# Loading v one chunk of four batches at a time from the GpSimd queue, in a fused linear-attention and SoLU kernel

## The chip, the cores and the metric

The kernel runs on one core of one Trainium2 chip. The core has five engines that run their own instruction lists and wait for each other by semaphores: TensorE (PE, matmuls; its weight loads are shown as PEld), VectorE (DVE), ScalarE (ACT), GpSimd (POOL) and SyncE (SP, which here only issues transfers). Sixteen DMA engines move data between the memory of the chip (HBM) and the on-chip memory (SBUF). The metric is the device time of one execution in microseconds (us).

## The reference

Two parts, one after the other. The first is a linear attention with decay, for 4 batches, 8 heads, 768 positions and a head size of 48; the second is a feed-forward layer with a softmax-gated unit and a layer norm, on the 3072 rows of 384 values that the first gives.

```python
for t in range(S):
    kt, vt, rt, wt = (k[:, :, t], v[:, :, t], r[:, :, t], w[:, :, t])
    cur = np.einsum('bhd,bhe->bhde', u[None] * kt, vt)
    y[:, :, t] = np.einsum('bhd,bhde->bhe', rt, state + cur)
    state = wt[:, :, :, None] * state + np.einsum('bhd,bhe->bhde', kt, vt)
...
h = x @ w_in
sm = e / (np.sum(e, axis=-1, keepdims=True) + 1e-09)     # e = exp(h - max)
solu = h * sm
ln = (solu - mu) / np.sqrt(var + 1e-06) * g_ln
return (ln @ w_out).astype(np.float32)
```

The arrays r, k, v and w are fp32 of shape (4, 8, 768, 48). For one batch and one chunk of 128 positions, v is 128 x 8 x 48 values, or 196,608 bytes, and lies in HBM in runs of 48 values (192 bytes), one for each position and head.

## The kernel before

The 768 positions are cut into 6 chunks of 128, and one chunk of one batch is a *unit*: unit i is batch i mod 4 of chunk i div 4, 24 units in all. A unit goes through some forty steps, and the whole program is one list, ORDER, in which each word is a step with its unit: `vb9.a` is the step `vb` of unit 9, on ACT (`.p` is POOL, `.d` is DVE; a digit is the PSUM bank). Each engine issues its own steps in the order of that list (the class `InOrder`), so an engine that waits for one step holds up all its later ones, whatever they need.

The steps that matter here, by their words:

- `LW`, `LK`, `LR`, `LV`: SP loads w, k, r and v of one unit, four transfers of 1024 runs of 192 bytes. Each goes into one of seven tiles (`NIO`), whose rows hold a head's 48 values in 64 places. `LI`, `LO` load the two weight matrices, `out` stores a finished unit; SP issues these too, 127 transfers in all.
- `vb` (function `v_cast`): casts a unit's v to bf16, on POOL for 12 units, on ACT for 6 and on DVE for 6. The bf16 tiles `vb` are a ring of ten.
- `p`, `q`, `qh` (POOL) and `dg` (DVE): the products of r, k and u, summed over a head. `dv` (POOL) is that sum times v.
- `lw` (ACT), `cum` (PE), `ex` (ACT), `kp` (DVE), `krk`, `krr` (PE), `kr`: k and r with their decays, turned for the matmuls.
- `M` (PE), `m` (ACT or DVE), `sel` (POOL, for the m that ACT copied): the scores of a unit and their mask. `Y` (PE) multiplies them with v; `y` copies the result, on DVE with dv added.
- `S` (PE) and `st` (DVE): the state that a batch's next chunk needs; S reads the cast v.
- `X`, `H` (PE), `e` (ACT), `he` (DVE), `ea` (POOL), `hq`, `Oa`, `Ob` (PE), `sq` (ACT), `qm` (DVE), `lv` (ACT, two instructions: the logarithm and the exponential that make 1/sqrt), `o`: the second part.
- `gw`, `mn`, `mc`, `ce`: the scaling and centring of the second weight matrix, once, at some 27 to 43 us.

The words are laid out so that several units are under way on every engine at once. Units are not taken strictly in sequence: at the start unit 2 goes first, then 1, 0, 3, 4.

Of the kernel before, what the change touches and what calls it, by code (L numbers as in the profile page):

```python
# [8 lines left out]
F32 = mybir.dt.float32  # L9
BF16 = mybir.dt.bfloat16  # L10
# [11 lines left out]
LW2 LU0 ik0 lw2 hot5.4 cum2.0 LW1 lw1 us0.7 ih0 LW3 lw3 cum3.2 LR2 uc0 ex2 LK2 p2 LV2 vb2.p kp2 hot4.4 krk2.6 krr2  # L22
LR1 LK1 cum1.4 LW0 ex1 kp1 kr2.d hot1.0 S2.7 lw0 et2 LV1 vb1.d LW4 st2 p1 q1 hot2.0 krk1.1 krr1 q2 qh2 dg2 LG0
kr1.a M2.4 ex3 hot1.0 M1.6 m1.d dv2 LR0 LK0 p0 q0 cum0.0 ex0 lw4 cum4.6 ex4 kp0 krk0.1 krr0 LR3 gs0.0 gc0 dg1
m2.d Y2.i0 kr0.d LK3 p3 LR4 LV0 vb0.a dg0 dv1 kp3 Y1.i5 hot3.1 krk3.4 krr3 LK4 kp4 M0.2 m0.d krk4.1 y1.a X1.5
krr4 y2.a X2.0 dv0 xT2.d hot1.6 Y0.n7 y0.d kr3.a M3.2 hot1.0 X0.6 S1.4 p4 q3 kr4.a xT1.a xT0.a LI2 LI1 wi1.a
M4.0 m4.a et1 LI0 S0.5 et0 wi0.d m3.d LO1 wi2.p H1.6 e1 gw5.a H2.0 e2 H0.2 LO0 gw2.a q4 qh4 dg4 qh3 dg3 gw4.p
gw7.p LV3 vb3.p dv3 sel4 LW6 e0 gw6.d st1 LV4 vb4.p he1 lw6 dv4 gw1.d LW5 gw0.d gw3.d mn0.4 mc0 ce5.p ce6.p
Y3.i7 ce4.p he2 st0 he0 cum6.0 y3.a ce7.p hot1.5 X3.6 lw5 xT3.a ce3.d LK6 LR6 p6 Y4.n5 LR5 LK5 ce2.d hq0.a ex6
LW7 cum5.2 H3.6 p5 y4.d ex5 ce1.d ce0.d Oa0.5 kp6 krk6.1 krr6 S4.0 hq1.d Oa1.4 kp5 krk5.3 krr5 X4.2 Ob1 e3 he3  # L30
LV5 q6 q5 kr5.d hq2.a et4 st4 M5.6 kr6.a M6.0 xT4.d lw7 cum7.2 hq3.a sq1 m6.a m5.d dg5 vb5.d qm1 dv5 Ob0 ex7 sq0
qm0 S3.7 qh6 LR7 LK7 p7 kp7 et3 lv1 st3 lv0 H4.0 Y5.n6 y5.d LR9 LK8 o1.d e4 krk7.3 krr7 Oa2.2 he4 X5.7 q7 kr7.d
LW9 lw9 o0.a LK9 p9 LW8 lw8 S5.6 et5 cum9.4 ex9 Ob2 sq2 LR8 p8 st5 dg6 kp9 qm2 LV6 xT5.a LV9 vb6.p dv6 sel6
cum8.0 ex8 kp8 hq4.a LV7 LV11 out1 LW10 dg7 vb7.p dv7 Oa3.3 vb9.a lv2 H5.6 e5 M7.4 m7.d he5 q8 krk9.1 LK10 krr9
kr9.a S9.0 et9 Ob3 sq3 st9 q9 qm3 o2.a out0 ea5.p Y6.i5 y6.a LV8 LR10 Y7.n4 y7.d LW11 LW12 krk8.1 M9.6 lw10 lv3
X6.2 xT6.a m9.d o3.a krr8 LV10 out3 out2 kr8.d qh9 dg9 dg8 hq5.d cum10.4 ex10 kp10 S6.0 vb11.d et6 X7.2 xT7.a
st6 p10 vb8.d dv8 dv9 H6.6 e6 he6 H7.2 lw11 e7 he7 M8.4 m8.a Oa5.1 Y9.n0 Ob5 sq5 y9.d cum11.6 ex11 krk10.5 krr10
qm5 kr10.d S7.4 et7 st7 Oa4.3 hq6.d lv5 lw12 o5.a X9.2 sel8 Y8.i0 vb10.p y8.a LK11 LR11 kp11 xT9.d q10 dg10 p11
M10.4 m10.a sel10 S10.1 et10 st10 dv10 S8.0 et8 S11.7 et11 X8.6 xT8.a LK12 LW13 cum12.4 q11 ex12 lw13 st11 st8
Ob4 sq4 qm4 LW14 LR12 kp12 p12 lw14 lv4 o4.a out5 LK13 LV12 LR13 Y10.n2 dg11 y10.d H8.6 e8 krk12.1 krk11.0 krr11  # L40
krr12 kr12.d he8 kr11.a q12 qh12 cum13.4 H9.2 vb12.p S12.1 ex13 p13 q13 ea7.p dg12 kp13 dv11 LW16 LR14 LK14 e9
he9 et12 st12 M12.6 m12.a Oa6.0 X10.5 xT10.a krk13.4 krr13 kr13.a M11.6 m11.d ea8.p dv12 sel12 p14 cum14.2 ex14
q14 out4 Ob6 sq6 hq8.d M13.4 m13.d LV13 hq7.a LW15 lw15 lw16 kp14 vb13.d H10.6 dg13 qm6 LW18 lw18 Y11.n1 y11.d
Oa8.5 LK16 LR15 LR16 LK15 e10 he10 hq9.a krk14.4 Y12.i3 krr14 lv6 qh14 kr14.d p15 ea10.p dv13 LR18 LV14 vb14.p
q15 qh15 LK18 p18 Ob8 sq8 qm8 y12.a S13.2 et13 st13 o6.a lv8 X11.1 xT11.d cum16.6 ex16 X12.3 hq10.d LW19 kp16
Oa9.4 cum15.0 xT12.a Ob9 ex15 kp15 sq9 o8.a dg14 dv14 qm9 M14.2 m14.a sel14 krk16.7 Oa7.6 krr16 kr16.d lv9 o9.d
cum18.0 ex18 kp18 Ob7 LV15 S14.5 et14 st14 krk15.3 krr15 kr15.d LK19 Y13.i2 lw19 cum19.0 krk18.7 p16 q16 vb15.a
S15.4 y13.a sq7 qm7 dg15 X13.5 xT13.d ex19 LR19 kp19 lv7 o7.a q18 krr18 kr18.d H11.2 et15 st15 krk19.5 krr19
kr19.d LW17 lw17 cum17.0 e11 he11 ex17 ea11.p out8 LK17 LR17 p17 kp17 H12.6 e12 he12 hq11.a p19 H13.4 e13 Oa10.3
Y14.n2 M16.0 m16.a dg16 q19 dv15 y14.d ea12.p ea13.p M15.6 m15.d he13 Ob10 sq10 X14.2 out9 Oa11.1 LW20 qm10 lw20  # L50
cum20.6 hq12.d krk17.0 krr17 out6 out7 LV16 vb16.a dv16 xT14.a S16.2 LR20 ex20 LK20 dg18 et16 st16 lv10 o10.a
H14.4 e14 kp20 Ob11 sq11 kr17.d LK23 qm11 lv11 o11.a Oa12.2 krk20.3 krr20 kr20.a he14 sel16 Y16.n7 y16.d Y15.n6
y15.d M19.4 m19.a M18.0 m18.d Ob12 X15.7 xT15.a q17 hq13.d LV19 LW21 LV17 X16.3 xT16.a ea14.p vb19.a M17.4 m17.d
sq12 LK22 out10 qm12 dg17 qh19 vb17.p sel19 p20 hq14.a LW22 LV20 q20 qh20 dv17 M20.0 LV21 m20.d out11 LK21 H15.6
e15 he15 lw22 ea15.p H16.4 LV18 vb18.p dv18 LR21 p21 lw21 Oa14.3 Y17.n1 LR22 LV23 q21 dg19 dv19 Ob14 LR23 p23
p22 e16 he16 lv12 Oa13.0 LW23 o12.a out12 sq14 qm14 hq15.d vb20.a lv14 dg20 dv20 y17.d cum21.6 ex21 Ob13 cum22.4
sq13 ex22 LV22 vb22.p ea16.p o14.d out14 Y18.n2 y18.d Oa15.1 X18.3 qm13 kp22 lv13 xT18.d X17.2 xT17.a kp21 Ob15
sq15 qm15 S18.5 et18 st18 Y19.n4 y19.d lv15 o15.a out15 o13.a krk22.2 S17.3 et17 lw23 H18.6 e18 ea18.p hq16.d
vb21.d st17 Y20.n5 y20.d X19.4 xT19.d krr22 kr22.a H17.0 he18 hq18.d cum23.4 ex23 kp23 Oa16.3 e17 ea17.p he17
krk21.2 krr21 kr21.a H19.6 e19 krk23.5 X20.4 krr23 q22 qh21 vb23.p out13 xT20.a kr23.a he19 Oa18.2 Ob16 sq16  # L60
M21.0 q23 ea19.p qh23 dg22 dv22 m21.a sel21 qm16 lv16 M22.6 hq19.a M23.4 Ob18 sq18 dg21 H20.0 o16.a out16 m22.d
m23.d Oa19.7 Y22.n6 qm18 lv18 hq17.d Ob19 S19.5 dg23 dv23 e20 Oa17.4 y22.d X22.3 he20 et19 st19 xT22.d dv21
Y21.n6 Ob17 y21.d sq19 o18.a sq17 qm17 lv17 Y23.n1 out18 qm19 lv19 X21.0 xT21.d H22.2 o17.a e22 out17 ea20.p
y23.d H21.0 X23.5 xT23.a e21 hq20.d o19.d out19 Oa20.6 he22 hq22.d H23.4 e23 he21 hq21.d Ob20 sq20 qm20 lv20
o20.a out20 ea22.p Oa22.7 ea21.p Oa21.3 he23 hq23.d Ob22 sq22 qm22 lv22 Ob21 sq21 qm21 lv21 o21.d o22.a out22
out21 ea23.p Oa23.2 Ob23 sq23 qm23 lv23 o23.a out23
"""

NIO, NLW, NKP, NWK = 7, 10, 6, 4
# [24 lines left out]
def kernel(  # L94
# [26 lines left out]

    nc.scalar.preload_act_table_set("natural_log_exp_and_others")
# [27 lines left out]
    v_t = ring("v_in", NIO, [C, H, 64], F32)  # L150
# [4 lines left out]
    g_rows = consts.tile([KF, 128], F32)  # L155

# [57 lines left out]
    qm_t = ring("qm", NWK, [C, 1], F32)  # L214
    lv_t = ring("lv", NWK, [C, 1], F32)
# [30 lines left out]
    def load_w(i, x):  # L246
        sp.dma_start(out=w_t[i % NIO][:, :, :D], in_=rows_of(w, i))

    def load_k(i, x):
        sp.dma_start(out=kr_t[i % NIO][:, 0, :, :D], in_=rows_of(k, i))  # L250

    def load_r(i, x):
        sp.dma_start(out=kr_t[i % NIO][:, 1, :, :D], in_=rows_of(r, i))

    def load_v(i, x):
        sp.dma_start(out=v_t[i % NIO][:, :, :D], in_=rows_of(v, i))

    def load_u(i, x):
        sp.dma_start(out=u_row, in_=u.rearrange("(o h) d -> o (h d)", o=1))

    def load_g(i, x):
        sp.dma_start(out=g_rows, in_=moe_g_ln.rearrange("(ko ki) -> ko ki", ki=128))

    def load_w_in(j, x):
        sp.dma_start(out=win_f[:, j, :], in_=moe_w_in[j * 128:(j + 1) * 128, :])

    def load_w_out(j, x):
        part = slice(j * KF // 2, (j + 1) * KF // 2)
        sp.dma_start(out=wout_f[:, part, :],
                     in_=moe_w_out.rearrange("(ko ki) d -> ki ko d", ki=128)[:, part, :])  # L270
# [79 lines left out]
    def v_cast(i, x):  # L350
        copy = {"a": act.copy, "d": dve.tensor_copy, "p": pool.tensor_copy}[x]
        copy(out=vb_t[i % NLW], in_=v_t[i % NIO][:, :, :D])
# [24 lines left out]
    def transposed_copy(i, x):  # L377
        copy = {"a": act.copy, "d": dve.tensor_copy}[x]
        copy(out=kr_s[i % NKP], in_=live[i]["kr_ps"])

# [87 lines left out]

    def hidden(i, x):
        xT = xT_t[i % NWK]  # L470
        h_ps = live[i]["h_ps"] = bank([128, KF, C], F32, x, "h_ps")
        for f in range(KF):
            for j in range(KM):
                pe.matmul(h_ps[:, f, :], lhsT=win_sb[:, j, f * 128:(f + 1) * 128], rhs=xT[:, j, :],
                          start=(j == 0), stop=(j == KM - 1))

    def hidden_exp(i, x):
        act.activation(out=e_t[i % NWK], in_=live[i]["h_ps"], func=EXP)
# [7 lines left out]
    def hidden_mul(i, x):  # L486
        dve.tensor_mul(out=he_t[i % NWK], in0=live[i]["h_ps"], in1=e_t[i % NWK])
# [96 lines left out]
```

## Time and profile before

The median is 155.07 us over 2 runs (154.83 to 155.32). The profiled execution has a span of 152.4 us from its first to its last instruction; the remaining 2.7 us of a run lie outside it.

| engine | busy, us | share of the span | instructions |
|---|---|---|---|
| PE | 136.4 | 90% | 2093 |
| PEld | 105.5 | 69% | 2093 |
| DVE | 131.8 | 87% | 227 |
| ACT | 120.0 | 79% | 247 |
| POOL | 119.0 | 78% | 149 |

In 40 equal slices of the span (3.8 us each), busy tenths of PE and POOL, the share of the 16 DMA engines, and what they moved:

```
PE   6777598968999999999998999999799999999970
POOL 7268986799909994899999997799889979973600
DMA  3999999989979999989897989995998110112023
GB/s 76 218 216 211 217 334 377 254 175 223 216 151 216 220 204 229 206 177 224 194 203 144 228 195 275 199 199 136 241 205 210 63 45 4 44 63 103 4 79 127
```

A digit 9 is 90% or more. All transfers of the kernel go through one hardware queue: 104,802 packets and 26.75 MB, 77.4% of the engines' time; 100,314 of all packets are under 512 bytes. How long a transfer takes from its issue to its landing is given by the profile as a median: 3.7 us for w, k and r of a unit, 3.6 us for v, 2.6 us for a store.

### The profile page before, as it was taken

Reading aid. Unit: us, or ns where it says so; the run is one execution under the profiler, and the core shown is the slowest. Engines: PE = TensorE matmul, PEld = TensorE weight load, DVE = VectorE, ACT = ScalarE, POOL = GpSimd, SP = SyncE. Lnnn points to the kernel's source line nnn. Section 1 sums busy time; section 2 is a strip of 40 time slices with the busy share of each in tenths; the row PEclk is TensorE's granted clock in tenths of the full one; section 3 lists DMA queues with packets and bytes.
Section 4 is the critical chain, followed back from the end, with each engine's and each line's share of the span. In section 5 each row is a group of like instructions: output and inputs, shape, how many; then the busy total and the mean of one; then the engine's idle time right before and its main releaser. Section 6 shows DMA issues by size and latency. Waiting matters only on the chain.

```text
span 152.4 us, 5172 instructions
## 1 busy us (share of the span) xinstructions
PE 136.4 (90%) x2093; PEld 105.5 (69%) x2093; DVE 131.8 (87%) x227; ACT 120.0 (79%) x247; POOL 119.0 (78%) x149
## 2 busy tenths in 40 slices
PE   6777598968999999999998999999799999999970
PEld 1242365936778889779776689887686988889740
DVE  5029968899999999998999999999999999988940
ACT  4526648869888999799998889998988789938661
POOL 7268986799909994899999997799889979973600
PEclk9959969999999999999999999999999999999998
DMA  3999999989979999989897989995998110112023
GB/s 76 218 216 211 217 334 377 254 175 223 216 151 216 220 204 229 206 177 224 194 203 144 228 195 275 199 199 136 241 205 210 63 45 4 44 63 103 4 79 127
DMA packets 104825, 27.06 MB, mean 178 GB/s; under 512 B 100314, under 2 KB 104419, under 8 KB 104803
## 3 DMA queue, kind: packets, MB, share of 16 engines
q1 hardware_dynamic: 104802, 26.75, 77.4%
q8 instruction: 16, 0.26, 0.7%
q14 instruction: 7, 0.05, 0.1%
HBM read 22.03 MB, written 4.72 MB: 176 GB/s over the span
## 4 chain that ended last, share of the span: by engine, by line
PE 53%; DVE 23%; SPq 8%; ACT 6%; issue 3%; DMA 2%; POOL 1%; DVEq 0%; POOLq 0%
PE ps L86 53%; SPq L86 7%; DVE he L86 6%; DVE m L86 4%; DVE kp L86 4%; DVE w L86 3%; DMA kr_in<-in_k_dram 2%; DVE kr L86 1%; DVE hq L86 1%; DVE y L86 1%; DVE st L86 1%; ACT ps L86 1%; ACT o L86 1%; DVE dg L86 1%; ACT win_sb L86 1%
## 5 line engine op out<-in xcount | busy, mean ns | idle before, releaser
L86 PE MATMUL ps<-w,he 128*128 128x385 bf16 x192 | 44.5, 325 | 1.0 <-DVE w L86 0.7
L86 PE MATMUL ps<-xT,win_sb 128*128 128x128 bf16 x576 | 35.5, 219 | 1.1 <-DVE qm L86 0.8
L86 PEld LDWEIGHTS <-win_sb 128*128 128x128 bf16 x576 | 32.8, 98 | 2.2 <-DVE m L86 0.9
L86 PE MATMUL ps<-one_col,hq 128*128 128x1 bf16 x192 | 31.5, 164 | 0.0
L86 DVE TENSOR_TENSOR he<-ps,e 128x1024 bf16<-128x1024 f32 x24 | 29.1, 1214 | 1.6 <-ACT e L86 1.6
L86 DVE TENSOR_TENSOR kp<-ps,kr_in 128x768 bf16<-128x768 f32 x24 | 22.8, 951 | 7.7 <-DMA kr_in<-in_k_dram 4.9
L86 POOL TENSOR_TENSOR p<-kr_in 128x384 bf16<-128x384 f32 x24 | 24.7, 1038 | 4.5 <-DMA kr_in<-in_k_dram 4.2
L86 POOL TENSOR_TENSOR dv<-vb,dg 128x384 bf16<-128x384 bf16 x24 | 21.7, 907 | 7.5 <-DVE qm L86 3.6
L86 ACT ACTIVATE e<-ps 128x1024 bf16<-128x1024 f32 x24 | 24.5, 1021 | 3.1 <-PE ps L86 2.0
L86 POOL TENSOR_TENSOR ea<-e 128x512 bf16<-128x512 bf16 x17 | 20.0, 1181 | 6.4 <-ACT e L86 5.7
L86 POOL TENSOR_TENSOR q<-p,u_bc 128x384 bf16<-128x384 bf16 x24 | 22.2, 931 | 2.4 <-DVE dg L86 1.7
L86 ACT ACTIVATE ps<-ps 128x768 f32<-128x768 f32 x24 | 19.1, 799 | 5.1 <-PE ps L86 4.3
L86 PEld LDWEIGHTS <-kp 128*128 128x128 bf16 x272 | 17.5, 100 | 6.0 <-DVE kp L86 3.2
L86 PEld LDWEIGHTS <-he 128*128 128x128 bf16 x192 | 18.4, 96 | 4.0
L86 PEld LDWEIGHTS <-hq 128*128 128x128 bf16 x192 | 15.4, 96 | 8.3
L86 DVE TENSOR_TENSOR m<-ps,keep 128x1024 bf16<-128x1024 f32 x15 | 18.2, 1216 | 1.2 <-PE ps L86 1.0
L86 PE MATMUL ps<-ident,kp 128*128 128x128 bf16 x192 | 16.5, 227 | 1.6 <-POOL p L86 1.1
L86 DVE TENSOR_TENSOR hq<-he 128x1024 bf16<-128x1024 bf16 x15 | 13.4, 890 | 0.1
L86 ACT COPY kr<-ps 128x1024 bf16<-128x1024 bf16 x11 | 11.1, 1012 | 2.4 <-PE ps L86 2.4
L86 ACT ACTIVATE lw<-w_in 128x384 bf16<-128x384 f32 x23 | 11.7, 523 | 1.3 <-DMA w_in<-in_w_dram 1.3
L86 PEld LDWEIGHTS <-kr 64*128 64x128 bf16 (+1 forms) x272 | 10.2, 95 | 3.1 <-ACT kr L86 0.7
L86 PE MATMUL ps<-inv_col,ea 128*128 128x1 bf16 x68 | 11.2, 165 | 0.0
(90 smaller groups left out, 293.7 us busy)
## 6 DMA issues: line engine op xcount, KB each, us to landing
w_in<-in_w_dram SPq DMA_DIRECT2D x24, 192.0 KB, 3.7
kr_in<-in_r_dram SPq DMA_DIRECT2D x24, 192.0 KB, 3.7
kr_in<-in_k_dram SPq DMA_DIRECT2D x24, 192.0 KB, 3.7
v_in<-in_v_dram SPq DMA_DIRECT2D x24, 192.0 KB, 3.6
out_dram<-o SPq DMA_DIRECT2D x24, 192.0 KB, 2.6
win_f<-in_moe_w_in_dram SPq DMA_DIRECT2D x3, 512.0 KB, 6.4
wout_f<-in_moe_w_out_dram SPq DMA_DIRECT2D x2, 768.0 KB, 9.0
u_row<-in_u_dram SPq DMA_DIRECT2D x1, 1.5 KB
```

The costliest lines, as they stand in the source:

```text
L86: made = make(*args, **kwargs)
```

## The change

v is no longer loaded unit by unit from SP. One transfer, issued by GpSimd, brings a whole chunk, that is four units (all four batches), in fp32: 4096 runs of 192 bytes, 786,432 bytes. It goes into one of two tiles of 32 x 48 values a row, without the gaps of the old tiles, and chunk c uses tile c mod 2. The steps `vb` stay what and where they were, and read a quarter of the wide tile. In ORDER the 24 words `LV0` to `LV23` (units) give way to six words `LV0` to `LV5` (chunks).

```diff
-    v_t = ring("v_in", NIO, [C, H, 64], F32)
+    v_g = ring("v_in", 2, [C, B * H, D], F32)
+    v_t = [v_g[j // B % 2][:, j % B * H:(j % B + 1) * H, :] for j in range(NU)]
...
-    def load_v(i, x):
-        sp.dma_start(out=v_t[i % NIO][:, :, :D], in_=rows_of(v, i))
+    def load_v(c, x):
+        pool.dma_start(out=v_g[c % 2], in_=v.rearrange("b h t d -> t (b h) d")[c * C:(c + 1) * C])
...
-        copy(out=vb_t[i % NLW], in_=v_t[i % NIO][:, :, :D])
+        copy(out=vb_t[i % NLW], in_=v_t[i])
```

Where the six words stand in the new list, each with some words on either side:

```
LW2 LU0 ik0 LV0 lw2 ... LK2 p2 vb2.p
gw2.a q4 LV1 qh4 dg4 qh3 dg3 gw4.p gw7.p vb3.p dv3 sel4 ... vb4.p
q7 kr7.d LW9 lw9 o0.a LK9 LV2 p9 LW8 ... vb6.p dv6 sel6 ... vb9.a lv2 rs2 H5.6 e5
q10 dg10 LV3 p11 M10.4 m10.a sel10 ... vb12.p S12.1
e11 he11 ex17 LV4 ea11.p out8 ... vb16.a dv16
ea15.p H16.4 LV5 vb18.p dv18 ... hq15.d vb20.a lv14 rs14 dg20 dv20 y17.d cum21.6 ex21 ... o14.d out14 Y18.n2 y18.d Oa15.1 X18.3
```

All other words keep their order, except that `lv` is split: its second instruction gets a word of its own, `rs`, directly behind the `lv` of the same unit (or with one `st` between, which is DVE's). ACT's, DVE's and PE's instructions stand in the same order as before; SP has 103 transfers in place of 127, and POOL has six more instructions.

```diff
     def scale(i, x):
-        act.activation(out=lv_t[i % NWK], in_=sq_t[i % NWK][:, 1:2], func=LN, scale=1e-6 * DF * DF,
-                       bias=qm_t[i % NWK])
+        act.activation(out=lv_t[i % NWK], in_=sq_t[i % NWK][:, 1:2], func=LN,
+                       scale=1e-6 * DF if i in by_rows else 1e-6 * DF * DF, bias=qm_t[i % NWK])
+
+    def root(i, x):
         act.activation(out=rs_t[i % NWK], in_=lv_t[i % NWK], func=EXP, scale=-0.5)
```

The rest of the diff adds ways that this list does not use: a table from which a load's word could choose another queue (all of them leave it at SP), a second form of the hidden layer for units named by words `ht`, and transposes by DMA (`kt`, `xt`). No word of the list names one of them, so `by_rows` is empty, and they add only a few small tiles.

## The prediction

> **What bounds the kernel now.** I read four views. First the chain that ended last: on the page its shares by engine, then its pieces in order of time.
>
> ```profile
> PE 53%; DVE 23%; SPq 8%; ACT 6%; issue 3%; DMA 2%; POOL 1%; DVEq 0%; POOLq 0%
> ```
>
> ```profile
> 13.35 3.79 DMA kr_in<-in_k_dram
> ...
> 43.27 31.86 PE ps L86 x551
> ...
> 110.34 37.23 PE ps L86 x601
> ```
>
> (Start, length, what.) The first 17 us are SP's issues end to end and a k load's landing; later there are two stretches of 32 and 37 us in which TensorE never waits, with a DVE and ACT stretch between. POOL holds 1% of the chain. Whatever stops TensorE inside its two stretches therefore lengthens the run one for one. Secondly, busy times by stage, for the places where loads are put:
>
> ```profile
> core 0: us, PE busy (x) PEld busy (x) DVE busy (x) ACT busy (x) POOL busy (x), PEclk, DMA share, GB/s
> 4.00:13.00 9.00, 6.85 (x43) 3.40 (x43) 2.64 (x4) 3.44 (x8) 4.49 (x9) 0.81 1.06 211
> 48.00:57.00 9.00, 9.00 (x159) 7.14 (x155) 8.89 (x15) 8.75 (x22) 8.83 (x11) 1.00 1.01 217
> ...
> 114.00:123.00 9.00, 9.00 (x159) 7.54 (x156) 9.00 (x18) 7.50 (x20) 8.84 (x11) 1.00 0.49 138
> ```
>
> The DMA share is full at 211 to 217 GB/s: with this kernel's small packets that is all that the 16 engines give. Only late, at 114, is half free. POOL has 8.8 of 9 us filled in the middle. Thirdly, the v loads (issue on SP, ns min/median/max; then landing):
>
> ```profile
> L86 SPq DMA_DIRECT2D v_in<-in_v_dram x24: 378/760/4108, 5.0 to 114.8; - x24
> ...
> DMA to landing us min/median/max: 3.1/3.6/6.7
> ```
>
> Fourthly, the timeline. The new loads stand in POOL's order behind these instructions (the first stands at 3.23, before everything shown; the second behind the q that ends at 24.38):
>
> ```profile
> 47.79 0.91 POOL L86 TENSOR_TENSOR q<-p,u_bc 128x384 bf16<-128x384 bf16 x1
> ...
> 64.46 0.91 POOL L86 TENSOR_TENSOR q<-p,u_bc 128x384 bf16<-128x384 bf16 x1
> 65.33 1.46 POOL L86 TENSOR_TENSOR p<-kr_in 128x384 bf16<-128x384 f32 x1
> 67.13 1.09 POOL L86 TENSOR_SCALAR_AFFINE_SELECT m<-m 128x1024 bf16<-128x1024 bf16 x1 [0.34 <-ACT et L86]
> ...
> 113.22 1.15 POOL L86 TENSOR_TENSOR ea<-e 128x512 bf16<-128x512 bf16 x1
> ```
>
> and the casts that need them, with what follows, are these:
>
> ```profile
> 52.19 0.51 ACT L86 CAST vb<-v_in 128x384 bf16<-128x384 f32 x1
> ...
> 53.61 0.33 PE L86 MATMUL ps<-vb,kp 128*128 128x96 bf16 x4
> ...
> 113.93 0.51 ACT L86 CAST vb<-v_in 128x384 bf16<-128x384 f32 x1
> ...
> 116.02 0.60 DVE L86 TENSOR_SCALAR o<-ps,rs 128x384 f32<-128x384 f32 x1
> ```
>
> The casts at 52.19 and 113.93 are vb9 and vb20. The fifth load is placed behind two q that end at 93.73, the sixth behind ea15, which ends at 114.37: after the moment at which vb20 ran.
>
> **The change part by part.** *Taken from SP:* 24 issues of 0.76 us median. In the middle SP's issues are on no chain, so that is worth nothing there; at the start v2 and v1 (0.99 and 1.11 us, with gaps 2.2 us) go from ahead of k3, but the bytes remain, see below. *Without a price:* lv and rs as two words keep the order of ACT; DVE's, ACT's and PE's orders do not change. The queue table, dead branches and new small tiles run nothing. Before LV2 to LV5 the tile is long free (vb3 ends at 30.5 against 48.7, vb7 at 53.5 against 65.4, vb10 at 64.5 and vb8 at 61.3 against 93.7, vb15 at 90.6 against 114.4), so these loads wait for nothing.
>
> *Landing, L.* A load is 4 x 196,608 = 786,432 bytes in the same 192-byte pieces. At 214 GB/s (middle of 211 and 217) that is 3.7 us alone, 7.3 us when SP's queue takes every other packet. The fixed part: the shortest landing, 3.1 us, less 0.9 us for its own bytes, is 2.2 us. So L lies between 5.9 and 9.5 us. I take 8 for the first five (share full there, though SP has fewer loads left), 5.9 for the last (share 0.49).
>
> The Trainium skill, page "DMA: Bandwidth & Descriptors", section "Anatomy of one DMA", fits about 2.0 us plus bytes at 436 GB/s, which as an estimate makes L 3.8 us and my sum below 6 instead of 14 us. The trace disagrees: by that rule 192 KB takes 2.5 us, and no v load here landed in under 3.1.
>
> *GpSimd's issue, G.* No row shows one. 4096 pieces must be described, and I assume that POOL's next instruction stands behind it. Nearest row: SP issues 1024 pieces in 0.38 us at best and 0.76 in the median, so G is 1.5 to 3.0 us for four; SP's longest, 4.1 us, would make 16.4; towards zero if GpSimd merely hands it on. I take 3.0, the row of the median, and keep 0 and 16.4.
>
> *Place by place* (late = free time of POOL + L - start of the cast, less the slack behind it):
> - LV0, 3.23: lands at 11.2, vb2 ran at 8.73, 2.5 late. G is covered: behind the load stand the small fills of halves and off_blocks, and POOL idles 2.98 us before p2. After vb2 it idled 1.27 us before p1, leaving 1.2. On DMA, four units' v pass before k3 in place of two: 2 x 0.9 = 1.8 more, which eats SP's saving. These run in parallel; with some of each, +2.0.
> - LV1, 24.38: vb4 ran at 32.61, lands 32.4: in time. G is covered by POOL's 1.74 us of waiting for w_out and 3.62 us at 42 to 45. If that cover went, it would cost the 3.0. +0.
> - LV2, 48.71: vb9 at 52.19, 4.5 late, with 0.9 us between its end (52.70) and the state matmuls at 53.61. Behind it on ACT stand lv2, rs2, e5; TensorE stands too. +3.6. G alone would cost less: sel6 has 1.9 us to spare.
> - LV3, 65.37: vb12 at 72.42 is only 0.9 late with 0.4 to spare. Here G decides: POOL has 0.34 us idle, then the select that ends at 68.22, 0.59 before the matmuls at 68.81. 3.0 - 0.34 - 0.59 = +2.1.
> - LV4, 93.73: vb16 at 99.90 is 1.8 late, 0.9 spare; G less 0.77 and 0.81 idle and 0.42 in front of Y16 says the same. +1.0.
> - LV5, 114.37: lands at 120.3, vb20 at 113.93: ACT stands 6.4 us with lv14, rs14, ex21 behind it. o14 on DVE (116.02) wants rs14 (ended 115.07), 0.95 spare; y18 stands behind o14, and PE's transposes at 117.17 behind y18. +5.5.
>
> Sum 14.2 us: span 152.4 to 166.6. The timed median of before, 155.07, is 2.7 us above the profiled span, and I keep that: **169.3 us**. With L 5.9, G 1.5 it is 0 + 0 + 1.5 + 0.6 + 0 + 5.4 = 7.5, 162.6; with L 9.5 everywhere and G 4.8 (four issues of 1.2, the longest at the start) 2.7 + 0 + 5.1 + 3.9 + 2.8 + 9.0 = 23.5, 178.6.
>
> **Rivals.** *GpSimd's own issue is the bound.* If G is 10 us, six make 60 on a POOL that is busy for 119.0 of 152.4. Of its 33 idle us some 18 lie between the first load and the tail. 155.1 + 60 - 18 = 197; at 16.4, 235. For it: no row bounds what 4096 pieces cost GpSimd. Against: 16.4 comes from an SP issue that mostly waited. It decides from G of about 5. The skill's page "SBUF — State Buffer", section "Who interferes with whom", says that certain DVE copies lock GpSimd out while it writes descriptors; no run here shows it yet, and DVE is full in these windows, so it would add to this rival. Chance 0.2.
>
> *SP's relief wins (not slower).* If the pieces cost GpSimd under 0.9 us and the wide tile's unbroken 6 KB rows let them land in 4 us, LV2 to LV4 are hidden (3.5 + 0.9 = 4.4 is the point), the start gains its 2.2 us, and LV5 costs 4 + 0.4 - 0.95 = 3.5: 156.4; with LV5 hidden too, 152.9. For it: SP's issues are 8% of the chain. Against: the share of 1.06 at the start, where nothing is gained by issuing sooner. Chance 0.13.
>
> *Forecast*, waits of ACT and PE for late v: 0.67.
>
> **How the numbers follow.** Likeliest 169, its own range 162 to 179. The 8-in-10 range takes in half of the POOL-bound rival and the small end: 158 to 196, leaving some 0.1 on each side. Two per cent is 3.1 us (about what can be told from no change): under 152 is faster, up to 158.2 is the same. The relief rival lies almost all in the middle, so 0.10 for same and 0.03 for faster; the remaining 0.87 is slower.
>
> **What would show it.** Right: ACT idle in front of vb9 and vb20 with DMA v_in as the releaser, some 4 and 6 us, and TensorE idle inside its two stretches; POOL gaps of 3 us behind the two q; SP with 103 issues; 24,576 packets on a queue of GpSimd's. Wrong: landings under 5 us; POOL gaps of 10 us (then the first rival); k and r landing earlier in the first 17 us by 2 us (then the second).

## The result, and the profile after

The changed kernel takes 175.05 us (median of 2 runs, 174.02 to 176.07) against 155.07 us: a ratio of 1.129, with a 95% interval of 1.113 to 1.146. Its profiled execution, the one of 174.02 us, has a span of 172.3 us against 152.4, so 1.7 us lie outside it. (The 2.7 us that the prediction kept are the median of before less the span of one profiled execution; in the later rounds the kernel before, too, takes some 1.7 us more than its span.) The forecast was 169.3 us, from 158 to 196. All times are medians of fast runs: a run that is over 1.5% above the fastest of its kernel is left out.

The page of the changed kernel: slices of the span (4.3 us each) with TensorE's busy tenths and granted clock, the two queues (q1 is SP's, q0 GpSimd's) with packets, MB and share of the 16 engines, and the chain by engine.

```profile
PE   5919488968999399999888999679891599999970
PEclk9999969999999969999999999999998599999996
q1 hardware_dynamic: 79842, 22.03, 55.5%
q0 software_dynamic: 1248, 4.72, 11.6%
PE 27%; DMA 23%; DVE 18%; POOL 18%; ACT 6%; issue 4%; SPq 2%; DVEq 0%; POOLq 0%; ACTq 0%
```

Before the change the granted clock was, in slices of 3.8 us:

```profile
PEclk9959969999999999999999999999999999999998
```

PE's row has holes in slices 2, 13, 25 and 26, 30 and 31 (counted from 0), where before it was at 9 from slice 10 to the tail but for an 8 and a 7. TensorE's share of the chain fell from 53% to 27%; transfers hold 23% (before 2%) and GpSimd 18% (before 1%). Busy times rose by 9.6 us on GpSimd, about what its six issues take (10.6), by 4.8 on PE and by less than 1 on DVE and ACT: most of what was added is waiting. The pieces of the chain, in order of time (start, length, what):

```profile
4.34 7.25 DMA kr_in<-in_k_dram
...
52.32 7.55 DMA v_in<-in_v_dram
...
73.53 8.30 DMA v_in<-in_v_dram
...
103.21 8.83 DMA v_in<-in_v_dram
...
126.23 6.96 DMA v_in<-in_v_dram
135.35 31.68 PE ps L85 x499
```

The first piece is k of unit 2, which took 7.25 us; the other four are the wide loads LV2 to LV5, each waited for until it landed. Of TensorE's two unbroken stretches only the last remains. The wide loads themselves (GpSimd's issue, ns min/median/max, first and last start; then landing):

```profile
L85 POOL DMA_DIRECT2D v_in<-in_v_dram x6: 1732/1742/1862, 3.2 to 126.2; - x6
...
DMA to landing us min/median/max: 7.0/7.9/8.8
```

Busy times by stage, around LV2's and LV5's landings, where before PE had 9.00 of 9 us:

```profile
core 0: us, PE busy (x) PEld busy (x) DVE busy (x) ACT busy (x) POOL busy (x), PEclk, DMA share, GB/s
...
52.00:61.00 9.00, 5.97 (x91) 4.55 (x89) 5.74 (x9) 4.84 (x12) 8.81 (x11) 0.95 0.81 184
...
126.00:135.00 9.00, 3.30 (x43) 2.10 (x41) 2.91 (x7) 1.75 (x6) 8.83 (x11) 0.82 0.44 109
```

PE, DVE and ACT stand together while GpSimd works on, and the DMA share is not full: it is the time of one transfer that is waited for.

And the timeline at the waits, with the idle time before an instruction and what ended it. First three of these instructions before the change, then those after it:

```profile
7.77 0.96 DVE L86 TENSOR_TENSOR kp<-ps,kr_in 128x768 bf16<-128x768 f32 x1 [4.67 <-DMA kr_in<-in_k_dram]
...
54.11 1.21 DVE L86 TENSOR_TENSOR he<-ps,e 128x1024 bf16<-128x1024 f32 x1
...
99.90 0.50 ACT L86 CAST vb<-v_in 128x384 bf16<-128x384 f32 x1
```

```profile
11.72 0.96 DVE L85 TENSOR_TENSOR kp<-ps,kr_in 128x768 bf16<-128x768 f32 x1 [8.62 <-DMA kr_in<-in_k_dram]
...
59.89 0.51 ACT L85 CAST vb<-v_in 128x384 bf16<-128x384 f32 x1 [3.94 <-DMA v_in<-in_v_dram]
...
61.78 1.23 DVE L85 TENSOR_TENSOR he<-ps,e 128x1024 bf16<-128x1024 f32 x1 [3.93 <-ACT e L85]
...
112.06 0.51 ACT L85 CAST vb<-v_in 128x384 bf16<-128x384 f32 x1 [2.54 <-DMA v_in<-in_v_dram]
...
133.22 0.51 ACT L85 CAST vb<-v_in 128x384 bf16<-128x384 f32 x1 [7.27 <-DMA v_in<-in_v_dram]
...
134.19 0.62 DVE L85 TENSOR_SCALAR o<-ps,rs 128x384 f32<-128x384 f32 x1 [6.09 <-ACT rs L85]
```

The first line of each is kp2. The three ACT lines after the change are vb9, vb16 and vb20; the one before it is vb16. Behind each the wait is handed on: DVE's he stands for e5 (3.93 us), DVE's o14 for rs14 (6.09 us), since ACT, which makes both, stood in front of a cast.

**Where each microsecond was lost.** ACT and DVE run the same instructions in the same order in both kernels, so the start of an instruction after, less its start before, is the loss up to there. Which step a loss belongs to is read from where it grows:

| place, by the time before | loss so far, us | step | the step's own loss | forecast |
|---|---|---|---|---|
| 8 us, kp2 | 4.0 | LV0 | 4.0 | 2.0 |
| 48 us | 3.6 | LV1 | -0.4 | 0 |
| 54 us, he behind vb9 | 7.7 | LV2 | 4.1 | 3.6 |
| 56 us, y | 8.2 | (TensorE at half clock) | 0.5 | none |
| 78 us, m | 9.5 | LV3 | 1.3 | 2.1 |
| 102 to 104 us | 12.0 | LV4 | 2.5 | 1.0 |
| 116 us, o14 | 18.2 | LV5 | 6.2 | 5.5 |
| 128 us, he | 19.5 | (TensorE at half clock) | 1.3 | none |
| end of the span | 19.9 | tail | 0.4 | none |

### The profile page after: what moved, and what is told of

It reads as the page before. It is cut to its first block, busy times and chain, and to the rows that moved or that the text cites. A ratio compares the mean times of both kernels' runs of the same rounds, so it can differ in the third digit from the quotient of the medians.

```text
span 172.3 us, 5157 instructions
## 1 busy us (share of the span) xinstructions
PE 141.2 (82%) x2091; PEld 107.6 (62%) x2093; DVE 132.7 (77%) x227; ACT 120.5 (70%) x247; POOL 128.6 (75%) x155
## 3 DMA queue, kind: packets, MB, share of 16 engines
q0 software_dynamic: 1248, 4.72, 11.6%
## 4 chain that ended last, share of the span: by engine, by line
PE 27%; DMA 23%; DVE 18%; POOL 18%; ACT 6%; issue 4%; SPq 2%; DVEq 0%; POOLq 0%; ACTq 0%
PE ps L85 27%; DMA v_in<-in_v_dram 18%; POOL q L85 5%; DMA kr_in<-in_k_dram 4%; POOL dv L85 4%; POOL p L85 4%; DVE m L85 4%; DVE he L85 3%; DVE kp L85 3%; DVE w L85 2%; POOL ea L85 2%; POOL m L85 2%; SPq L85 2%; DVE dg L85 1%; ACT e L85 1%
## 5 line engine op out<-in xcount | busy, mean ns | idle before, releaser
L85 PE MATMUL ps<-w,he 128*128 128x385 bf16 x192 | 45.8, 332 | 1.5 <-DVE m L85 0.7
L85 POOL TENSOR_TENSOR dv<-vb,dg 128x384 bf16<-128x384 bf16 x24 | 20.8, 872 | 11.6 <-DVE vb L85 5.1
L85 PEld LDWEIGHTS <-he 128*128 128x128 bf16 x192 | 18.6, 97 | 4.1 <-issue 0.2
L85 PEld LDWEIGHTS <-kr 64*128 64x128 bf16 (+1 forms) x272 | 10.7, 98 | 3.3 <-issue 0.7
L85 DVE TENSOR_TENSOR st<-ps,et 128x384 bf16<-128x384 f32 x20 | 10.8, 546 | 2.6 <-ACT et L85 2.6
L85 ACT CAST vb<-v_in 128x384 bf16<-128x384 f32 x6 | 3.1, 510 | 13.7 <-DMA v_in<-in_v_dram 13.7
```

Of the source, the lines that this page charges most:

```text
L85: made = make(*args, **kwargs)
```

## The experiments

The theory, called A in the expectations: the wide loads are too late for their casts, because each stands in GpSimd's full list a landing time before its first reader or behind it; and the first one's bytes delay k2. The rivals: GpSimd's own time for describing 4096 pieces (B), and contention or layout of the wide transfers themselves (C). Some expectations set the letters anew. The ratio is in each case to runs of the kernel before on the same chip, with its 95% interval.

**The words earlier.** Four of the six words are moved up GpSimd's list; nothing else changes.

```diff
-LK9 LV2 p9 ... dg10 LV3 p11 ... ex17 LV4 ea11.p ... H16.4 LV5 vb18.p
+q6 q5 LV2 kr5.d ... p10 LV3 vb8.d ... sel12 LV4 p14 ... vb15.a LV5 S15.4
```

> Edit: LV2 to LV5 issued earlier in GpSimd's order (behind q5, p10, sel12 and vb15), LV0 and LV1 where they were. Late landing (theory A): the three long waits for v (3.9, 2.5 and 7.3 us on ACT) and the wait of vb12 go, with the half clock that followed the longest; only the start's 4 us are left, so a ratio to the kernel before of 1.02 to 1.04 (158 to 161 us), and no wait for v above 1 us behind 40 us. GpSimd's own time (theory B): 6 x 1.74 us stay on POOL, so 165 us or more (1.065 and up). SP's loads held up by the wide ones (theory C): the same DMA work in other places, 168 or more, with waits for k, r and w in place of v.

Measured: 158.43 us, 1.021 (1.017 to 1.026). The loads take what they took in the changed kernel, and one short wait for v is left; in the trace's answer for the tile v_in, the issue on GpSimd, idle time by releaser, and landing:

```profile
L84 POOL DMA_DIRECT2D v_in<-in_v_dram x6: 1729/1750/1937, 3.2 to 97.2; - x6
...
  DMA v_in<-in_v_dram: 0.8, 1
...
DMA to landing us min/median/max: 7.0/8.4/8.9
```

Same issue time, about the same landing, and of the 20 us lost 3.2 are left (158.43 less 155.27). So the place in the list makes most of the loss, and not the fact that GpSimd spends 10.5 us on issuing (six times 1.75). What the issue time costs at the old places is not told apart here, since it moved too; a later run asks that. The expectation had only the start's 4 us left. The sum agrees, but not its parts: on DVE the loss is 4.1 us at kp2, 2.4 at 45 us, 4.3 at 85 and 3.9 at 121, so slack takes up part of the late start and something later adds about as much.

**Only the last word earlier.**

```diff
-H15.6 e15 he15 lw22 ea15.p H16.4 LV5 vb18.p
+vb15.a LV5 S15.4
```

> Edit: only LV5 is issued earlier (behind vb15). A: the wait of 7.3 us at vb20 and the half clock behind it go, 6 to 8 us, so 167 to 169 us, a ratio of 1.08 to 1.09. B and C: at most 2 us, 173 or more (1.115 and up).

Measured: 170.74 us, 1.100 (1.093 to 1.106), with a span of 168.7 us: 3.6 us shorter, where LV5's own loss was 6.2, and between what the two sides had expected. The chain of this run, in order of time, has:

```profile
50.91 7.99 DMA v_in<-in_v_dram
104.60 9.75 DMA v_in<-in_v_dram
```

Behind vb20 nothing is lost any more, but LV5 is now issued at 101.99 us, just ahead of LV4 at 104.60, and ACT's wait for vb16 grew from 2.54 to 6.48 us. Of these 3.9 us, 0.9 is LV4's longer landing (9.75 for 8.83), 1.4 its later issue (104.60 for 103.21), behind LV5's on GpSimd, and 1.6 that ACT comes to vb16 earlier. So here a word that was moved alone pushed the next one back.

**The same words, issued by SP.**

```diff
-        pool.dma_start(out=v_g[c % 2], in_=...)
+        sp.dma_start(out=v_g[c % 2], in_=...)
```

> Edit: the same six wide loads at the same places of the list, issued by SP in place of GpSimd; POOL has its 149 instructions of before. A: the landing counts and not who issues; about 6 to 8 us from issue to landing, SP comes by the places a little earlier than POOL, so 163 to 174 us (1.05 to 1.12), still with waits for v. B: POOL's 10 us are given back, 160 to 163. C, with GpSimd's queue taking more than its half of the DMA engines: k and r at the start are held up longer by a first-in first-out queue or not at all, DVE's first wait for k (8.6 us) changes by 2 us or more.

Measured: 158.3 us, 1.021 (1.016 to 1.026), outside what either theory gave. The issue and the landing on SP's queue:

```profile
L85 SPq DMA_DIRECT2D v_in<-in_v_dram x6: 389/698/853, 1.8 to 111.4; - x6
...
DMA to landing us min/median/max: 6.1/6.8/12.0
```

The last issue is at 111.4 where GpSimd came to it at 126.2. Even against the moments at which GpSimd was free in the kernel *before* (48.71, 65.37, 93.73 and 114.37), SP reaches the same four words 4.8, 1.9, 3.3 and 2.9 us earlier (43.89, 63.51, 90.42, 111.44): it has nothing to do but issue, so it runs ahead of the list. With the 4 us by which everything else starts late, that is enough for every landing: no engine waits for v. The start is lost as before: DVE waits 8.8 us for k2, here too. So the 4 us come with the wide load, whoever issues it. The Trainium skill, page "DMA: Bandwidth & Descriptors", section "Issuing engines are not separate DMA queues", states that all issuers share the same 16 engines and that their transfers interleave. The run agrees at the start.

**GpSimd's time by itself.** The kernel before, with two fills of 0.95 us each on GpSimd at the six places of the changed list; together they take 1.9 us, a little more than an issue. The loads are as before.

```diff
+    def spend(i, x):
+        pool.memset(spare[:, :1024], 0.0)
+        pool.memset(spare[:, 512:], 0.0)
```

> Edit: the kernel before, with two fills of a spare tile on POOL (together some 1.7 us) at each of the six places where the wide loads stand; no load is changed. A: some 1 to 2 us, only at the fourth and fifth place, 156 to 157.5 us (1.005 to 1.015). B: POOL's time is the cost, 163 us or more (1.05 and up).

Measured: 159.85 us, 1.029 (1.024 to 1.034): 4.6 us, between the two theories, more than A had allowed. GpSimd's time at these places does cost when nothing else is late. In the changed kernel the waits for v stand at the same places, so the two need not add; how much of the 20 us is GpSimd's time there, no run tells apart. From the table, LV3's 1.3 us are the one step put down to it.

**The first chunk by units.** Chunk 0 is loaded by four SP transfers (words `LF`) at the places of the kernel before; the other five words stay as changed.

```diff
-LW2 LU0 ik0 LV0 lw2
+p2 LF2 vb2.p ... et2 LF1 vb1.d ... LR4 LF0 vb0.a ... gw7.p LF3 vb3.p
```

> Edit: the changed kernel, but its first chunk comes as four unit loads from SP at the places of before, into the quarters of the wide tile; LV1 to LV5 as in the change. If the 4 us at the start come from the three other units' bytes ahead of k2 and k1, they go and nothing else: 170 to 172 us, ratio 1.095 to 1.11, DVE's first wait for k back to 4.7 us. If they come from GpSimd's queue being live beside SP's at any time, or from tile sizes: 174 to 176.

Measured: 170.49 us, 1.107 (1.098 to 1.115). Until 32 us nothing is late by more than half a microsecond; at 116 us the loss is 14.8 and at 128 us 16.0. So the start's 4 us come from the wide load being under way ahead of k2.

**Both, and what was left.** Early words and a first chunk by units.

> Edit: first chunk from SP as in the run before it, and LV2 to LV5 issued early as in the first experiment; LV1 in its place. If landing and start are all of the loss: 153.5 to 156 us, ratio 0.99 to 1.005, five wide loads on GpSimd notwithstanding. If GpSimd's 5 x 1.75 us cost anything by themselves: 157 or more (1.01 and up).

Measured: 157.47 us, 1.024 (1.018 to 1.030; 1.021 against the mean of all eleven runs of the kernel before in that round). That is no better than the run with the early words alone, though the start's 4 us are gone, so the first of the two outcomes expected did not come. The loss on DVE grows later instead, from 0.7 us at 30 to some 3 at 85, as it does in the other run from 2.4 at 45 to 4.3 at 85. Waits for v come to 2 us. Two runs then asked what it was: wide loads 1 to 5 from SP, so that GpSimd issues nothing; and the kernel before with fills of 1.7 us on GpSimd at those five early places.

> The wide loads of chunks 1 to 5 issued by SP, at the changed kernel's words of the list, and the first chunk by four unit loads of SP at the places of the kernel before; GpSimd issues nothing. Theory A (late landings, the bytes ahead of k2 and k1 at the start, and GpSimd's own time at five places): all three are gone, so 154 to 157 us, a ratio of 0.99 to 1.01, no wait for v over 1 us. Theory B (a wide transfer costs by sharing the engines with w, k and r wherever it stands): it stays within 1 us of the run in which SP issued all six, that is 157 to 158.5, with k or r late in the middle.

> The kernel before, and at the places of the five wide loads of the run with early words and a first chunk by units, two memsets of together 1.7 us on GpSimd in place of the issue; no load is changed. Theory A (what that run still lost, 2.4%, is GpSimd's time at these five places): 157 to 159 us, a ratio of 1.015 to 1.03. Theory B (it is the wide transfers' share of the engines): 155 to 156, under 1.01.

Measured: 157.13 us, 1.019 (1.015 to 1.022) for the first, and 155.24 us, 1.005 (1.002 to 1.008) for the second. Both go by theory B and against A: GpSimd's time at the *early* places costs 0.8 us in all, and without any GpSimd issue most of the loss stays. The first differs from the run before it in the places too, which are the changed kernel's, so it is not a test of the issuer alone. Its trace shows one place where time goes: SP issues LV2 at 42.95 us and an r at 48.13, GpSimd's step p waits for that r, and the loss on DVE grows from 0.9 us at 37 us to 3.8 at 58.

```profile
53.62 1.00 POOL L84 TENSOR_TENSOR p<-kr_in 128x384 bf16<-128x384 f32 x1 [3.04 <-DMA kr_in<-in_r_dram]
```

In the version with both, and in the first of these two, ACT's steps lw behind the first wait for late w 3.9 and 4.1 us, in four waits each, where before it is 1.3 in two. The longest is at 32 us, next to LV1. So the second chunk was put back to unit loads too, once with GpSimd issuing chunks 2 to 5 and once with SP:

```diff
-gw2.a q4 LV1 qh4
+st1 LF4 vb4.p ... he3 LF5 q6 ... qm2 LF6 xT5.a ... hq4.a LF7 out1
```

> The run with early words and a first chunk by units, and also the second chunk by four unit loads of SP at the places of the kernel before; GpSimd issues four wide loads (chunks 2 to 5). Theory A (what was still lost, 2.4%, is mostly the second wide load's bytes ahead of w, at some 24 to 32 us, where ACT waits 2.1 us for a w): 155 to 156.2 us, a ratio of 1.002 to 1.01, and the shift at 32 us gone. Theory B (each wide load costs some half us wherever it stands): 156.5 to 157, a ratio of 1.013 to 1.02.

> The run in which SP issues the wide loads and a first chunk by units, and also the second chunk by four unit loads; SP issues four wide loads at the changed kernel's words. Theory A: 155 to 156, a ratio of 1.0 to 1.01, and no k late at 32 to 48 us. Theory B: 156 to 157, a ratio over 1.01. Faster than the kernel before by neither.

Measured: 156.18 us, 1.010 (1.006 to 1.013), and 155.97 us, 1.007 (1.003 to 1.010). ACT's longest wait for w, in the timeline of the version with both, where the first chunk alone comes by units:

```profile
34.92 0.52 ACT L84 ACTIVATE lw<-w_in 128x384 bf16<-128x384 f32 x1 [2.13 <-DMA w_in<-in_w_dram]
```

and the same step in that with the first two by units and GpSimd issuing the rest:

```profile
32.62 0.53 ACT L84 ACTIVATE lw<-w_in 128x384 bf16<-128x384 f32 x1
```

The wait is gone; the medians are 1.2 to 1.3 us lower (157.47 to 156.18, 157.13 to 155.97) and the ratios 1.2 to 1.4% (1.024 to 1.010, 1.019 to 1.007). So the second wide load costs 1 to 2 us too, where the start is not late already. That it does so by the late w is not shown: between the two traces ACT gains 2.3 us at this lw, but from 43 us on ACT and DVE run at the same times in both, to within 0.4 us, and their spans differ by 0.5 us (155.8 and 155.3). With two chunks by units and four wide, 0.7 to 1.0% remain. In the first one's trace the loss on DVE grows from 0.7 to 1.3 us at 58 us, behind a wait of 0.79 us for an r, and by another 1.6 at 78 to 86 us, next to the issue of LV4; the fills alone lose 0.5 us there. No run takes these apart.

**The transfer converts.** The version with both, but the five wide loads write bf16 straight into the tiles vb; twenty casts go.

```diff
-        pool.dma_start(out=v_g[c % 2], in_=...)
+        pool.dma_start(out=vb_g[c % 3], in_=...)
```

> Edit: as the run before it, but the five wide loads convert to bf16 on their way, into three wide tiles from which the matmuls read, so 20 of the 24 casts are gone (10 on POOL, 5 on ACT, 5 on DVE, some 10 us of engine time). If TensorE's own work is the floor by now: within 1 us of the run before, 0.98 to 1.0. If the shared load of DVE, ACT and POOL still sets the middle: 150 to 153 us, 0.965 to 0.985. If the converting load lands later or takes GpSimd longer: waits for v, over 157.

Measured: 158.07 us, 1.027 (1.021 to 1.034), no better than with the casts. GpSimd's queue (packets, MB, share) in the converting run:

```profile
q0 software_dynamic: 20560, 1.97, 23.5%
```

and in the run that it was made from:

```profile
q0 software_dynamic: 1040, 3.93, 10.2%
```

Half the bytes are written, but there is now about one packet for each piece of 192 bytes read, and the engines are held for over twice the time. The landing went to a median of 11.7 us, and the steps that read vb wait for it by 3.8 us in all.

**Four unit transfers in place of each wide one.** The early words, but each is four GpSimd transfers.

```diff
+        for b in (2, 1, 0, 3) if c == 0 else range(B):
+            pool.dma_start(out=v_t[c * B + b], in_=rows_of(v, c * B + b))
```

> Edit: the first experiment (early places), but each wide load is four transfers of one unit, one behind the other on GpSimd, unit 2 first in the first chunk. If GpSimd pays by the piece: 0.44 us an issue, four together 1.75 us as before, and 156.5 to 159 us; v of unit 2 is there early, but k2 still shares the engines, so the start stays 3 to 4 us late. If it pays by the transfer: 1 to 1.7 us each, 17 to 30 us more on POOL in all, 163 us or more.

Measured: 163.74 us, 1.067 (1.058 to 1.075). The issue and the landing:

```profile
L84 POOL DMA_DIRECT2D v_in<-in_v_dram x24: 882/886/1147, 3.2 to 103.2; - x24
...
DMA to landing us min/median/max: 3.4/5.0/6.3
```

Each lands sooner, nothing waits for v, and with unit 2 first kp2 is only 1.1 us late. But four issues take 3.5 us of GpSimd at a place where the wide one takes 1.75, 22.1 us in all, and the loss grows to 6.3 at 102 and 9.1 at 121 us. GpSimd holds 34% of the chain that ended last: here its own time is the bound.

## Why the prediction was right, and where its steps were off

The sign and the mechanism hold, and so do the two largest terms, LV5 and LV2, in their order; the span came out 5.7 us above the sum (172.3 against 166.6). Four of the six steps came out larger than forecast, and only LV3 clearly smaller, so the figure was not saved by errors that cancel.

- **Landing, L.** 7.0 to 8.8 us, median 7.9; 8 was taken. The rule of the Trainium skill that was weighed against it (page "DMA: Bandwidth & Descriptors", section "Anatomy of one DMA"; 3.8 us by estimate) did not hold here, with 192-byte pieces and SP's queue at work. The Trainium skill's fit is for loads that GpSimd issues, and the prediction held SP's against it; the run with four unit transfers has GpSimd's own, 3.4 us at the least where the rule gives 2.5. With the prediction's G of 3.0, its own terms make 6.4 to 7.5 us by that rule, and not "below 6". The last load took 6.96 where 5.9 was taken, which is 1.1 us more in LV5.
- **GpSimd's issue, G.** 1.74 us; 3.0 was taken, and the bounds 1.5 to 3.0 held; so the gaps of 3 us foreseen behind the two q are issues of 1.74. The far end of 16.4 came from an SP issue that mostly waited, as was said.
- **LV0** was mis-sized by half, 4.0 for 2.0. The step let v pass ahead of k3, by the order of SP's one queue. But the load is issued at 3.20 on a second queue and is under way when SP issues k2 at 4.34; k2 took 7.25 us (before, kp2 started 3.7 us after k2's issue), and kp2, not vb2, ends the wait. So "these run in parallel, some of each" named the wrong transfer. The run with a first chunk by units showed it.
- **LV1** at nothing was right in this kernel (-0.4). With the start mended the second wide load costs 1 to 2 us; by what path is open.
- **LV2**, 4.1 for 3.6. 4.5 late and 0.9 us of slack were reckoned; the slack was read at the state matmuls. It is not there for lv2, rs2 and e5, which stand behind the cast on ACT, nor for he behind e5: DVE idles 3.93 us. The right slack is that of the waiting engine's next instruction.
- **LV3**, 1.3 for 2.1, "G decides": with G at 1.74 the same sum gives 0.8, and vb12 waits 0.31 us for the landing besides.
- **LV4**, 2.5 for 1.0, from the same step: 0.9 us of slack was reckoned, but xT14 stands right behind vb16 on ACT and TensorE waited 2.33 us for it; and the load took 8.83.
- **LV5**, 6.2 for 5.5: the path by rs14 and o14 is as described, and the later landing (1.1 us) covers the difference.
- **Not forecast:** 1.8 us in the two stretches after a stall in which TensorE ran at half clock (put down to the clock from their place alone), and 0.4 in the tail.
- **Rivals.** GpSimd's issue as the bound needed G of 5; it was 1.74, and this rival is refuted. The lock-out of GpSimd by DVE copies that was to add to it (the Trainium skill, page "SBUF — State Buffer", section "Who interferes with whom") was not seen: no issue of a wide load in any run took over 1.94 us. Whether such a copy ran on DVE during an issue, no run shows. SP's relief is refuted: no wide load of the changed kernel landed in under 7.0 us, and k2 came 4 us later, not 2 earlier.
- **What would show it.** ACT idle before vb9 and vb20 was named as 4 and 6 us and is 3.94 and 7.27; SP's transfers are 103. The packets were wrong: 1248, not 24,576, which makes 208 to a load and about 20 pieces (4 x 1024 / 208) to a packet.

Of the whole 20 us, some 17 go when the words are early: the late landings and what follows from them, with an unknown part for GpSimd's time at the late places. The terms don't add: 4 us gained at the start gave 3.5 us with the late words (the loss at 128 us fell from 19.5 to 16.0), but 1.0 us of the span with the early ones (156.8 to 155.8), where slack had already taken up part of the late start by 45 us. No version tried was faster than the kernel before.

## What to carry to other kernels

Merging loads saves issues, but it moves the bytes of what is needed last ahead of what is needed first, and its landing grows with the size (a median of 5.0 us for one unit from GpSimd, 7.9 to 8.4 for four); so a merged load must be issued a landing time (here 8 us) and a margin before its first reader, and the first loads of a kernel are best left small. Before moving an issue to a computing engine, look up when that engine *reaches* the place in its list: here SP, which only issues, came by the words 1.9 to 4.8 us ahead of GpSimd, which was full. And count the slack of a late operand at the next instruction of the engine that waits, not only at the operand's readers.

## What the runs showed of the hardware

- **Packing.** The plain wide load goes as 208 packets for 4096 pieces of 192 bytes, the same load with a conversion as about one packet a piece, and holds the engines for over twice as long (23.5% against 10.2%), though it writes half the bytes.
- **Cost of an issue on GpSimd.** 0.886 us for 1024 pieces and 1.742 for 4096, both medians: by a straight line through the two, as an estimate, 0.60 us and 0.285 us for each 1024 pieces. A wide load's issue took 1.72 to 1.94 us at every place in every run that has one.
- **The clock after a stall.** The row PEclk of the changed kernel has 6, 6, and 8 with 5 in slices 5, 14, and 30 with 31, behind or beside stalls of TensorE; the trace's clock record has half speed for 3.4 us at 22.6 and 60.2 and for 6.8 at 131.8. The kernel before has such pieces only in its first 22 us and its tail. The run with the early words has one only in its tail (its record begins at 18.6 us), though its first wait for k is as long (8.8 us): not every stall is followed by such a piece. The Trainium skill, page "TensorE: Matmul & The Clock Gate", section "Part 1: The HAM clock gate", states a free-running activity window of some 3.4 us; one and two such windows agree with these pieces. The 1.8 us put down to it are read from where the loss grows, not from a run that changed the clock alone.
